# A fused attention and mixture-of-adapters kernel: moved key/value rows, moved counts, exchanged PSUM banks and a new order of the last chunks

## The chip, the cores and the metric

The kernel runs on one core of one Trainium2 chip. The metric is the time of one execution on the device in microseconds (us); the median of several runs is compared. All times inside an execution come from one profiled execution and count from the start of its span.

## The reference

Attention over spatially pooled keys and values, and then a mixture of low-rank adapters on its result. q is 4 x 12288 x 128 (batch, rows, channels) and kv is 4 x 384 x 32 x 128.

```
kv_pool = kv.reshape(B, H//4, 4, W//4, 4, C).mean(axis=(2, 4))   # 768 rows per batch
k = v   = kv_pool.reshape(B, 768, C) @ w_sr
x       = softmax(q @ k.T / sqrt(C)) @ v
logits  = x @ w_gate                        # 8 experts
w       = softmax over the two largest logits
out     = x + sum over these two e of  w[e] * (x @ A[e]) @ B[e]   # A[e] 128x16, B[e] 16x128
```

x has 4 x 12288 = 49152 rows; all inputs and the output are fp32.

## The kernel before

**The chunks.** The rows of q are handled in 96 chunks of 512 rows, 24 to a batch. The source numbers batches from 0; the words "batches 3 and 4" mean those with the numbers 2 and 3, the last two. One pass of the main loop (line 686, `for c in range(2, NCH - 1)`) does one stage for each of several chunks, so that each engine always has work: scores of a chunk ahead, weighing of chunk c-1, the turn of x of chunk c-2, and the adapters of a chunk some 6 to 9 back. The order of instructions on each engine is the order in which the source issues them (the scheduler is manual), and an instruction waits in its engine's queue until its operands and its buffer are ready; everything behind it on this engine waits too.

**One chunk, in order.** SyncE (SP) issues the loads of q and their transposes. TensorE (PE) does three times two score matmuls (`next_scores`, line 628; matmuls L329), each pair into one of two "sg" buffers of two PSUM banks, and ScalarE makes exp of them (L330). PE weighs values with these exponentials (`weigh`, L341, 24 matmuls in two halves) into the pair of banks "x". The values carry eight columns more: seven hold the gate logits relative to the eighth, and a column of ones gives the softmax's sum. VectorE (DVE) normalises x of the chunk (reciprocal L348, multiplication into `xn_all` L352) and takes the largest logits (MAX8, L359). GpSimd (POOL) makes the argument of the gate from them (L368 to L372) and casts q (L108). PE turns the upper halves of x into bf16 columns (`turned`, L408) in the bank "tp", and VectorE copies them out (`evacuate`, L419).

**The adapters.** ScalarE makes tanh of the gate's argument, VectorE transposes it (`send_gates`, L428), SP stores it to a buffer `g_h` in DRAM (L429), and `load_gates` (L436) loads it back, repeated over the adapters' 16 rows, as `ge`. `gated_hidden` multiplies x with A (L443, one matmul into the bank "hd" or one that is given) and VectorE multiplies with the gates, into `ht` (L446). `up` multiplies `ht` with B (L489, four matmuls, `d_ps`, into "hd" or a bank that is given); `give` adds x on VectorE (L503) and SP stores a pair of chunks (L522). In a usual chunk PE's order is: scores, first half of the weighing, scores, `up` of an old chunk into "hd", second half of the weighing, a step of key/value preparation if one is due, the turn of x into "tp", scores, `gated_hidden` into "hd".

**The lag.** `LAGS` (line 675) says how many chunks later the hidden layer of a chunk runs: 9 at first, then 8 from chunk 57, 7 from chunk 67, 6 from chunk 81. Where the lag falls, a pass has two hidden layers (65, 74 and 87) or two up-projections (69, 78 and 91). The loop issues the additional one in the place of the up-projection (lines 704 to 707), and one of the two takes the bank "tp":

```
for x in made.get(c, ())[:-1]:
    gated_hidden(x, t_bank())
for x in ups.get(c, ()):
    up(x, None if x == ups[c][-1] else t_bank())
```

**PSUM.** All eight banks are taken in the loop: "tp" and "hd" one buffer of one bank each, "x" one buffer of two banks, "sg" two buffers of two banks.

**Keys and values.** `plan(b)` (line 279) writes, by hand, in which pass the twelve rows of kv of a batch are loaded by SP (`at`; `load_row`, L87, 512 KB each), summed on POOL (`sm`; L194, L198 and L199), and pooled, made values and keys on PE and ScalarE (`st`; L210, L218, L226), relative to the first pass of the batch before. `prep` (rows and sums) comes near the end of a pass, `prep_step` after the weighing. POOL's `squares` (L265, L269) and VectorE's `ranges` (L272, L273) sum the squares of values and of gate columns, for a test of their size. `count_ok` (L553, L555, L558), `values_ok` (L561 to L563) and `count_sum` (L568 to L572) count in passes 82 to 86 whether all softmax sums and values so far are in the range that the fast formulas need; `ranges` stand in passes 32, 40, 56 and 80. All of these stand ahead of the last `gated_hidden` of a pass and of VectorE's copy of x.

**The last chunks.** After the loop the source issues the rest by hand (lines 757 to 909, n = 95 is the last chunk), with other banks, and with the gates applied by token instead of by row (`gate_args`, `gate_tanh`, `gate_w`, `gated`). `x_first` puts x into the bank of an up-projection by four small matmuls with the identity (L481), in which case ScalarE only copies the sum out (`take`); without it VectorE adds x (`add_rows`, L503). The last chunk is handled in two halves: two rows of tokens by `x_first` and ScalarE, two by VectorE. `all_ok` (L580 to L584) makes the flag `bad`, which every engine reads; a slow general path under `tc.If(bad_v != 0)` isn't taken here.

## Time and profile before

| What | Value |
|---|---|
| Median of the three runs shown | 374.38 us |
| Lowest and highest of them | 373.61 and 374.59 us |
| The profiled execution's own time | 374.13 us |
| Its span (first to last instruction) | 372.2 us |
| Mean granted TensorE clock | 0.999 |
| Passes of the main loop | 93 (chunks 2 to 94) |

The profile gives for each engine the busy share of the span, the chain of work that ended last, and groups of instructions by source line. In a row of the timeline, the first number is the start in microseconds from the start of the span, the second the busy time, then come engine, source line, operation, output<-inputs, shape and count, and in brackets how long the engine stood idle before it and what released it. "SPq" is SyncE issuing a transfer, "DMA" the transfer itself. Rows that count (x12) hold that many instructions in one.

### The profile page before, as it was taken

The numbers are of one execution on the slowest core, as the hardware profiler recorded it, in microseconds if no ns is written. First come the engines' busy times: TensorE is split into PE (matmuls) and PEld (weight loads), VectorE is DVE, ScalarE is ACT, GpSimd is POOL, SyncE is SP. The second block draws the span as 40 slices with busy tenths as digits, with TensorE's granted clock in tenths as the row PEclk, the third lists the DMA queues.
The fourth block names the chain that finished last, engine by engine and source line by source line (L and its number), as shares of the span: only waits on it lengthen the run. The fifth ranks groups of instructions, "written<-read, shape, count | busy, mean of one in ns | idle before, by whom it ended". The sixth has DMA issues, their size and how long they took to land.

```text
span 372.2 us, 10593 instructions
## 1 busy us (share of the span) xinstructions
PE 357.0 (96%) x3945; PEld 263.1 (71%) x3945; DVE 300.3 (81%) x953; ACT 308.8 (83%) x390; POOL 223.5 (60%) x374
## 2 busy tenths in 40 slices
PE   3889999999999899999999999999999999999985
PEld 1556777777777677777777777777777777677773
DVE  3785558888888788888888888888888889988994
ACT  1679998989889798988988988988888888879844
POOL 1022799988799787755679787755534324323243
PEclk9999999999999999999999999999999999999999
DMA  7999999999999999999999999998778799745324
GB/s 275 421 342 228 308 302 308 304 319 298 293 349 319 278 303 335 230 326 309 306 302 375 273 333 283 258 308 236 242 210 269 225 229 238 223 119 142 146 114 173
DMA packets 83818, 101.01 MB, mean 271 GB/s; under 512 B 58804, under 2 KB 59060, under 8 KB 83764
## 3 DMA queue, kind: packets, MB, share of 16 engines
q1 hardware_dynamic: 83332, 99.98, 94.3%
q8 instruction: 31, 0.51, 0.6%
q10 hardware_dynamic: 432, 0.33, 0.3%
q14 instruction: 23, 0.19, 0.2%
HBM read 62.33 MB, written 25.90 MB: 237 GB/s over the span
## 4 chain that ended last, share of the span: by engine, by line
PE 87%; DVE 5%; DMA 3%; ACT 3%; issue 1%; POOL 1%; SPq 0%; ACTq 0%; DVEq 0%
PE xps L341 34%; PE sg L329 31%; PE t_ps L408 5%; PE d_ps L489 5%; PE h_ps L443 5%; PE w_ps L609 2%; DMA ge<-g_h 2%; ACT tt L330 2%; PE v_ps L218 1%; DMA w_gate_sb<-in_moe_w_gate_dram 1%; DVE xn_all L352 1%; DVE ht L446 1%; DVE osb L503 1%; PE k_ps L243 1%; ACT qT L597 0%
## 5 line engine op out<-in xcount | busy, mean ns | idle before, releaser
L330 ACT ACTIVATE tt<-sg 128x1024 f16<-128x1024 f32 x288 | 276.9, 1022 | 36.5 <-PE sg L329 35.5
L329 PE MATMUL sg<-qT,kfT 128*128 128x512 f16 x576 | 170.2, 379 | 0.5 <-ACT qT L597 0.3
L341 PEld LDWEIGHTS <-tt 128*128 128x128 f16 x2304 | 146.1, 98 | 28.4 <-DVE xn_all L352 18.1
L341 PE MATMUL xps<-vext,tt 128*128 128x136 f16 x2256 | 164.7, 223 | 0.3 <-DVE xn_all L352 0.2
L503 DVE TENSOR_TENSOR osb<-d_ps,xn_all 128x512 f32<-128x512 f32 x85 | 58.7, 691 | 28.9 <-PE d_ps L489 27.8
L368 POOL TENSOR_TENSOR arg<-xn_all,top 128x64 f32<-128x64 f32 x47 | 14.4, 306 | 100.2 <-DVE top L359 80.6
L352 DVE TENSOR_TENSOR xn_all<-xps,rinv_all 128x540 f32<-128x540 f32 x94 | 67.7, 720 | 3.3
L329 PEld LDWEIGHTS <-kfT 128*128 128x128 f16 x576 | 49.2, 98 | 24.6 <-issue 1.8
L194 POOL TENSOR_TENSOR kvt<-kvt 128x1024 f32<-128x1024 f32 x27 | 63.6, 2357 | 2.7 <-DMA q<-in_q_dram 2.6
L108 POOL CAST q<-q 128x1024 f16<-128x1024 f32 x45 | 46.8, 1040 | 23.4 <-DMA q<-in_q_dram 23.4
L446 DVE SCALAR_TENSOR_TENSOR ht<-ge,h_ps 128x512 bf16<-128x512 f16 x87 | 58.5, 673 | 1.9 <-DMA ge<-g_h 1.4
L489 PEld LDWEIGHTS <-ht 128*128 128x128 bf16 x368 | 27.0, 98 | 25.1 <-DVE ht L446 6.1
L359 DVE MAX8 top<-xn_all 128x8 f32<-128x8 f32 x376 | 35.0, 156 | 6.3
L419 DVE COPY xt<-t_ps 128x512 bf16<-128x512 bf16 x92 | 36.8, 400 | 0.0
L408 PE MATMUL t_ps<-id_bf,xn_all 128*128 128x128 bf16 x376 | 36.3, 219 | 0.0
L489 PE MATMUL d_ps<-b_bf,ht 128*128 128x128 bf16 x340 | 32.9, 219 | 1.2 <-DVE ht L446 1.2
L443 PE MATMUL h_ps<-xt,a_bf 128*128 128x512 bf16 x87 | 33.0, 379 | 0.1
L348 DVE RECIPROCAL rinv_all<-xps 128x4 f32<-128x4 f32 x94 | 17.1, 182 | 12.9 <-PE xps L341 11.5
L408 PEld LDWEIGHTS <-xn_all 128*128 128x128 bf16 x376 | 25.9, 98 | 0.3
L371 POOL TENSOR_SCALAR msk<-msk 128x64 f32<-128x64 f32 x47 | 20.1, 428 | 4.1
L372 POOL TENSOR_TENSOR arg<-arg,msk 128x64 f32<-128x64 f32 x47 | 15.0, 319 | 3.9
L370 POOL TENSOR_TENSOR arg<-arg,msk 128x64 f32<-128x64 f32 x47 | 15.0, 319 | 3.7
(152 smaller groups left out, 220.4 us busy)
## 6 DMA issues: line engine op xcount, KB each, us to landing
kvt<-in_kv_dram SPq DMA_DIRECT2D x48, 512.0 KB
q<-in_q_dram SPq DMA_DIRECT2D x46, 512.0 KB
out_dram<-osb SPq DMA_DIRECT2D x44, 512.0 KB
ge<-g_h SPq DMA_DIRECT2D x45, 256.0 KB
out_dram<-osb SPq DMA_DIRECT2D x7, 256.0 KB
q<-in_q_dram SPq DMA_DIRECT2D x1, 1024.0 KB
qT<-q SPq DMA_TRANSPOSE x46
g_h<-g_sb SPq DMA_DIRECT2D x45, 16.0 KB
```

Source lines behind the costliest of these rows:

```text
L108: nc.gpsimd.tensor_copy(q16[i], q32[i].rearrange("p k n -> p (k n)"))
L194: eng.tensor_tensor(v[:, 0], v[:, 0], v[:, d], op=ALU.add)
L329: mm(sg[:, k], kfT[b][:, j * P:(j + 1) * P], qc, start=True, stop=True)
L330: nc.scalar.activation(tt[c][:, 2 * r:2 * r + 2], sg, AF.Exp, bias=0.0, scale=scale)
L341: mm(o, tt[c][:, j, s * P:(s + 1) * P], vext[b][:, j, 0:VW], start=(j == 0 and s % 2 == 0), stop=(j == NJ - 1 and s % 2 == 1), skip_group_ ...
L352: nc.vector.tensor_tensor(xn[c][:, :, 0:C + G].rearrange("p (b s) v -> p b s v", b=2), xv[:, :, :, 0:C + G], ri.rearrange("p (b s) -> p b ...
L408: mm(columns(t_ps, c, s), src[:, s], id_bf, is_transpose=True, start=(s == 0), stop=(s == NS - 1), skip_group_check=True)
L419: nc.vector.tensor_copy(to, t_ps)
L443: mm(h_ps, a_bf, xT[c], start=True, stop=True)
L446: nc.vector.scalar_tensor_tensor(hgT[c].rearrange("p (k a) t -> p k (a t)", k=2), gE[c // 2][:, h:h + NS // 2].rearrange("p a t k -> p k ( ...
L489: mm(dps[c][:, s], columns(hgT[c], c, s), b_bf, start=(s == 0 and fresh), stop=(s == NS - 1), skip_group_check=True)
L503: nc.vector.tensor_tensor(osb[:, lo:hi], d, xn[c][:, lo:hi, 0:C], op=ALU.add)
```

## The change

There are four edits.

1. In `plan`, for the batches with the numbers 2 and 3, the rows of kv are loaded, summed and used two passes later (`sm`, `st`); the loads (`at`) lie two passes apart, but for one pair (the ninth and tenth row, in the same pass). The passes of `squares` move by two as well (`k0`).
2. `ranges`, `count_ok`, `values_ok` and `count_sum(1)` come at the end of a pass, behind the last `gated_hidden`, `send_gates` and VectorE's copy of x.
3. In a pass with two hidden layers, the first goes to "hd" and the up-projection that follows to "tp" (before: "tp" and "hd"). In a pass with two up-projections, the first goes to "hd" and the second to "tp" (before: "tp" and "hd").
4. After the loop: chunk n-2 gets its x by `x_first`, two rows of tokens early and two late, and is copied out by ScalarE; the gate of chunk n runs on VectorE (`last_args`, `gate_w`) but for its mask on POOL; one turn is split into its matmuls (`turned_in`) and its copy (`fetch`); chunk n isn't halved any more: `up(n)` goes to "tp", VectorE adds x to all of it, and one store follows on ScalarE's queue; `all_ok` comes last, in the bank "hd".

```diff
@@ -283,9 +283,9 @@
             sm = [3, 5, 6, 8, 9, 10, 12, 14, 16]
             st = [10, 14, 19]
         else:
-            at = [-11, -9, -7, -5, -5, -3, -1, 1, 1, 3, 5, 7]
-            sm = [-3, -1, 1, 3, 5, 7, 9, 11, 13]
-            st = [4, 10, 16]
+            at = [-9, -7, -5, -3, -1, 1, 3, 5, 7, 7, 9, 11]
+            sm = [-1, 1, 3, 5, 7, 9, 11, 13, 15]
+            st = [6, 12, 18]
         for i, k in enumerate(at):
             loads.setdefault(c0 + k, []).append((b, i // 4, i % 4))
         for i, k in enumerate(sm):
@@ -701,10 +701,11 @@
         next_scores()
         if c in tanhs:
             gate_tanhs(tanhs[c])
-        for x in made.get(c, ())[:-1]:
-            gated_hidden(x, t_bank())
+        two = len(made.get(c, ())) > 1
+        if two:
+            gated_hidden(made[c][0])
         for x in ups.get(c, ()):
-            up(x, None if x == ups[c][-1] else t_bank())
+            up(x, t_bank() if two or x != ups[c][0] else None)
             give(x)
         if c in fetched and lag(2 * fetched[c] + 1) <= 8:
             load_gates(fetched[c])
@@ -722,20 +723,11 @@
             _, evacuate_h = turned("h", c - 4, stile("t_ps")[:, 0])
         next_scores()
         prep(c)
-        k0 = 19 if b == 0 else 17
+        k0 = 19
         if k in (k0, k0 + 2, k0 + 4) and b + 1 < B:
             if b == 0:
                 squares(0, (k - k0) // 2)
             squares(b + 1, (k - k0) // 2)
-        if c in (32, 40, 56, 80):
-            ranges((32, 40, 56, 80).index(c))
-        a = slice(0, CUT * NS)
-        if CUT < c <= CUT + 3:
-            count_ok(a, c - CUT - 1, flags[:, 0:1])
-        elif c == CUT + 4:
-            values_ok()
-        elif c == CUT + 5:
-            count_sum(1)
         for x in made.get(c, ())[-1:]:
             gated_hidden(x)
         if c in sent:
@@ -747,6 +739,16 @@
         if c == NCH - 2:
             evacuate_h(True)
 
+        if c in (32, 40, 56, 80):
+            ranges((32, 40, 56, 80).index(c))
+        a = slice(0, CUT * NS)
+        if CUT < c <= CUT + 3:
+            count_ok(a, c - CUT - 1, flags[:, 0:1])
+        elif c == CUT + 4:
+            values_ok()
+        elif c == CUT + 5:
+            count_sum(1)
+
 
 
     score_banks.close()
@@ -767,6 +769,17 @@
         eng.tensor_tensor(a, a, m, op=ALU.add)
         eng.tensor_scalar(m, m, 0.0, None, op0=ALU.is_ge)
 
+
+    def last_args():
+        lg = xn[n][:, :, C:C + E]
+        bc = [P, NS, E]
+        t1, t2 = (top5[:, :, i].unsqueeze(2).broadcast_to(bc) for i in range(2))
+        nc.gpsimd.tensor_tensor(msk5, lg, t2, op=ALU.subtract)
+        nc.gpsimd.tensor_scalar(msk5, msk5, 0.0, None, op0=ALU.is_ge)
+        nc.vector.tensor_tensor(arg5, lg, t1, op=ALU.subtract)
+        nc.vector.tensor_tensor(tmp5, lg, t2, op=ALU.subtract)
+        nc.vector.tensor_tensor(arg5, arg5, tmp5, op=ALU.add)
+
     def gate_tanh(lo, hi, arg):
         nc.scalar.activation(arg[:, lo:hi], arg[:, lo:hi], AF.Tanh, bias=0.0, scale=0.5)
 
@@ -786,19 +799,23 @@
             hb.rearrange("p s (r e) -> p s r e", e=E),
             g[:, lo:hi].unsqueeze(2).broadcast_to([P, hi - lo, RK, E]), op=ALU.mult)
 
-    def turn(src, lo, hi, bank_, store, key, act=True):
...
+    def turned_in(src, bank_):
...
+    def fetch(t_ps, store, key, act=True):
...
+    def turn(src, bank_, store, key, act=True):
+        fetch(turned_in(src, bank_), store, key, act)
     def high(c):
         return xn[c].bitcast(U16)[:, :, 1:2 * C:2].bitcast(BF16)
@@ -816,8 +833,9 @@
     top4, top5 = top[:, 0:NS], top[:, NS:2 * NS]
     pair = xn_all[:, q_ % 5]
     xn[n - 1], xn[n] = pair[:, 0:NS], pair[:, NS:2 * NS]
-    arg4, msk4, arg5, msk5 = (
-        small.tile([P, NS, E], FP32, tag=f"r{i}", name=f"r{i}", bufs=1) for i in range(4))
+    arg4, msk4, arg5, msk5, tmp5 = (
+        small.tile([P, NS, E], FP32, tag=f"r{i}", name=f"r{i}", bufs=1) for i in range(5))
+
     def tops4(c, top, y):
         ri = rinv_all[:, c]
         xv = y[:, :, 0:2 * VW].rearrange("p b (s v) -> p b s v", v=VW)
@@ -851,6 +869,7 @@
     up(n - 6, bank(1))
     o6 = take(n - 6)
     h2 = hidden(n - 3, 0, NS, mtile([P, NTOK], name="h2"))
+    x_first(n - 2, fbank(0), 0, 2)
     up(n - 5, bank(0))
     gate_args(n - 1, 0, NS, nc.gpsimd, top4, arg4, msk4)
     y5 = ps_e.tile([P, 2, 512], FP32, tag="y5", name="y5")
@@ -859,7 +878,7 @@
     put(n - 5, add_rows(n - 5))
     add(n - 6, o6, nc.gpsimd)
     put(n - 6, o6)
-    turn(high(n - 1), 0, NS, bank(1), xT, n - 1)
+    turn(high(n - 1), bank(1), xT, n - 1)
     h3 = hidden(n - 2, 0, NS, t_bank())
     gated(n - 2, 0, NS, gw[q_ - 1][:, NS:2 * NS], h3)
     weigh(n, 1)
@@ -869,44 +888,36 @@
     gate_w(0, NS, nc.gpsimd, arg4, msk4)
     tops4(n, top5, y5)
     tail_ok()
-    turn(hg[n - 3], 0, NS, mtile([P, NTOK], name="t2"), hgT, n - 3)
+    turn(hg[n - 3], mtile([P, NTOK], name="t2"), hgT, n - 3)
     h4 = hidden(n - 1, 0, NS, bank(1))
-    turn(hg[n - 2], 0, NS, t_bank(), hgT, n - 2)
-    turn(high(n), 0, NS, bank(0), xT, n)
-    gate_args(n, 0, NS, nc.gpsimd, top5, arg5, msk5)
+    last_args()
+    t_3 = turned_in(hg[n - 2], t_bank())
+    turn(high(n), bank(0), xT, n)
+    x_first(n - 2, None, 2, 4)
+    up(n - 3, mtile([P, NTOK], name="d2"))
     gate_tanh(0, NS, arg5)
-    up(n - 3, mtile([P, NTOK], name="d2"))
-    x_first(n - 1, fbank(1), 0, 2)
+    fetch(t_3, hgT, n - 2)
     gated(n - 1, 0, NS, arg4, h4)
-    up(n - 2, fbank(0))
-    put(n - 3, add_rows(n - 3))
-    put(n - 2, add_rows(n - 2))
+    gate_w(0, NS, nc.vector, arg5, msk5)
     x3 = ps_e.tile([P, 2, 512], FP32, tag="y5", name="x3")
     h5 = hidden(n, 0, NS, x3[:, 0])
-    turn(hg[n - 1], 0, NS, bank(1), hgT, n - 1)
-    gate_w(0, NS, nc.gpsimd, arg5, msk5)
     gated(n, 0, NS, arg5, h5)
-    x_first(n - 1, fbank(1), 2, 4)
+    add(n - 4, o1, nc.gpsimd)
+    put(n - 4, o1)
+    put(n - 3, add_rows(n - 3))
+    turn(hg[n - 1], bank(1), hgT, n - 1)
+    x_first(n - 1, fbank(1), 0, 2)
+    up(n - 2)
+    o3 = take(n - 2)
+    put(n - 2, o3)
+    turn(hg[n], bank(0), hgT, n, False)
+    x_first(n - 1, None, 2, 4)
     up(n - 1)
     o4 = take(n - 1)
     put(n - 1, o4)
-    add(n - 4, o1, nc.gpsimd)
-    put(n - 4, o1)
-    d5 = as_tokens(x3[:, 1])
-    for s in range(2):
-        mm(d5[:, s], id_f32, xn[n][:, s, 0:C], start=(s == 0), stop=False, skip_group_check=True)
-    turn(hg[n], 0, 2, bank(0), hgT, n)
-    turn(hg[n], 2, 4, t_bank(), hgT, n, False)
-    all_ok(bank(1))
-    for s in range(2):
-        mm(d5[:, s], hgT[n][:, s], b_bf, start=False, stop=(s == 1), skip_group_check=True)
-    o5 = half_out()
-    nc.scalar.activation(o5[:, 0:2], d5[:, 0:2], AF.Copy)
-    d6 = as_tokens(mtile([P, NTOK], name="d6"))
-    for s in range(2, 4):
-        mm(d6[:, s - 2], hgT[n][:, s], b_bf, start=(s == 2), stop=(s == 3), skip_group_check=True)
-    nc.vector.tensor_tensor(o5[:, 2:4], d6[:, 0:2], xn[n][:, 2:4, 0:C], op=ALU.add)
-    put(n, o5, queue=nc.scalar)
+    up(n, t_bank())
+    put(n, add_rows(n), queue=nc.scalar)
+    all_ok(mtile([P, NTOK], name="cnt"))
 
     end_banks.close()
     ps_g = ctx.enter_context(tc.tile_pool(name="ps_g", bufs=1, space=bass.MemoryType.PSUM))
```

18 lines of the change are left out of this document (9 added, 9 removed).

## The prediction

> **What bounds the kernel now.** I read the page from the top, then the chain of work that ended last, then the timelines of PE, DVE and SP around the chunks that the edits touch.
>
> ```profile
> span 372.2 us, 10593 instructions
> PE 357.0 (96%) x3945; PEld 263.1 (71%) x3945; DVE 300.3 (81%) x953; ACT 308.8 (83%) x390; POOL 223.5 (60%) x374
> PEclk9999999999999999999999999999999999999999
> DMA  7999999999999999999999999998778799745324
> PE 87%; DVE 5%; DMA 3%; ACT 3%; issue 1%; POOL 1%; SPq 0%; ACTq 0%; DVEq 0%
> ```
>
> PE sets the pace: it holds 87% of the chain, and its clock is never cut. The DMA engines are nearly full until about two thirds of the span. So an edit pays only where PE waits, and such waits must be looked for one by one. A chunk in which nothing waits looks like this (I call the start of the chunk's first weighing matmul W; the next W is 281.97, quoted below):
>
> ```profile
> 278.59 0.87 PE L341 MATMUL xps<-vext,tt 128*128 128x136 f16 x12
> 279.74 0.39 PE L489 MATMUL d_ps<-b_bf,ht 128*128 128x128 bf16 x4
> 280.16 0.69 DVE L503 TENSOR_TENSOR osb<-d_ps,xn_all 128x512 f32<-128x512 f32 x1 [0.40 <-PE d_ps L489]
> 281.08 0.72 DVE L352 TENSOR_TENSOR xn_all<-xps,rinv_all 128x540 f32<-128x540 f32 x1
> ```
>
> The reader is to see: d_ps at W+1.15, VectorE's add at W+1.57 after 0.40 us of idle, xn_all done at W+3.21, the next W at W+3.38. PE is back to back, and VectorE has some tenths to spare. Every chunk that takes over 3.38 us plus its own extra matmuls has a wait in it.
>
> **The change part by part.** *1. The kv rows.* The one long PE wait of the loop:
>
> ```profile
> 120.39 6.86 DMA ge<-g_h
> ...
> 127.34 0.69 DVE L446 SCALAR_TENSOR_TENSOR ht<-ge,h_ps 128x512 bf16<-128x512 f16 x1 [1.43 <-DMA ge<-g_h]
> ...
> 126.31 0.59 PE L329 MATMUL sg<-qT,kfT 128*128 128x512 f16 x2
> 128.09 0.40 PE L489 MATMUL d_ps<-b_bf,ht 128*128 128x128 bf16 x4 [1.18 <-DVE ht L446]
> ...
> 105.17 0.57 SPq L436 DMA_DIRECT2D ge<-g_h  x1
> 111.66 0.58 SPq L436 DMA_DIRECT2D ge<-g_h  x1
> 113.44 1.45 SPq L87 DMA_DIRECT2D kvt<-in_kv_dram  x2
> 120.39 0.59 SPq L436 DMA_DIRECT2D ge<-g_h  x1
> ```
>
> d_ps should follow the start of the two sg matmuls by 0.43 us (they are 0.216 apart), so at 126.74; it came at 128.09: 1.34 us lost. It waited for ht, ht for the gates' load, and that load was issued late: SP passed from one gates load to the next in 6.5 us where one kv row lay between, and in 8.7 us where two did (113.44), while two chunks of PE take 6.8 and, with a pooling step in them, a little more. One row in two chunks keeps pace; each second row costs about 1.5 us of lead. The old plan has such pairs in chunks 13 (with the batch before), 19 and 25; the new one has none before chunk 31, so three rows fewer, some 4.5 us of queue, lie ahead of the load that was 1.4 us late. I take this wait as gone: **-1.34**. What is late next: the pair in chunk 31 and the rows in 33 and 35, where the old plan had none; they give the lead back only in part, since the total of rows issued is at no chunk above the old total. Bounds: -1.34 and 0. Each moved row, an SP issue of about 0.6 us, is put behind two more chunks' gates, q, transposes and output stores, which pass it by. Around batch 4's rows no wait for a load stands now, and they move the same way. The sums on POOL move with the pooling on PE; for the later rows the lead of a load over its sum shrinks from six chunks to four, 13.5 us, twice what the late gates load took to land (6.86). Pooling, value and key steps, and the squares on POOL, move by two chunks; their work stays the same.
>
> *2. The counts behind the copy.*
>
> ```profile
> 317.14 0.87 PE L341 MATMUL xps<-vext,tt 128*128 128x136 f16 x12
> 317.36 0.48 DVE L555 SCALAR_TENSOR_TENSOR ok<-rinv_all,ok 128x324 f32<-128x324 f32 x1
> 317.76 0.68 DVE L446 SCALAR_TENSOR_TENSOR ht<-ge,h_ps 128x512 bf16<-128x512 f16 x1
> 318.50 0.40 PE L489 MATMUL d_ps<-b_bf,ht 128*128 128x128 bf16 x4
> ...
> sum 17.72, DVE 16.50; mean DVE 3.30
> ```
>
> The count stands ahead of ht; h_ps's bank comes free only at 318.44, and d_ps starts at W+1.36 instead of W+1.15. The last row is the sum of the five chunks that hold such a wait and no other extra (three with ranges, two with counts): 17.72 - 5 x 3.38 = 0.82 us. A sixth, with the flags of the values, has the same order beside two small matmuls of its own; I count it as the mean of the five, 0.16. All of that, 0.98, of which I take **-0.95**, goes when ht and the copy come first. What covers the counts then is VectorE's idle time ahead of the add (0.40 in a chunk without a gates transpose, about 0.25 with one). The longest, 0.48 to 0.5 us, overruns it by about 0.1 to 0.2; xn_all would end at W+3.3 to 3.4, and the next weighing needs it some 0.05 before W+3.38. So up to 0.05 comes back in each chunk: bounds -0.98 and -0.65.
>
> *3. The banks at lag changes.* Six chunks have a second hidden layer (65, 74, 87) or a second up-projection (69, 78, 91).
>
> ```profile
> 281.97 0.87 PE L341 MATMUL xps<-vext,tt 128*128 128x136 f16 x12
> 282.20 0.67 DVE L446 SCALAR_TENSOR_TENSOR ht<-ge,h_ps 128x512 bf16<-128x512 f16 x1
> 282.91 0.38 DVE L419 COPY xt<-t_ps 128x512 bf16<-128x512 bf16 x1
> 283.35 0.38 PE L443 MATMUL t_ps<-xt,a_bf 128*128 128x512 bf16 x1
> 283.76 0.69 DVE L446 SCALAR_TENSOR_TENSOR ht<-ge,t_ps 128x512 bf16<-128x512 f16 x1 [0.47 <-PE t_ps L443]
> 284.37 0.68 DVE L503 TENSOR_TENSOR osb<-d_ps,xn_all 128x512 f32<-128x512 f32 x1
> 284.50 0.38 PE L408 MATMUL t_ps<-id_bf,xn_all 128*128 128x128 bf16 x4
> 285.95 0.88 PE L341 MATMUL xps<-vext,tt 128*128 128x136 f16 x12
> ...
> sum 23.21, DVE 19.69; mean DVE 3.28
> ```
>
> Today the first hidden layer waits for the copy out of the "tp" bank: 283.35 instead of 283.12, 0.23 late. With the exchange it goes to the "hd" bank, free at 282.87, and that wait is gone. But "tp" is then held by the up-projection, whose reader is the *second* VectorE operation of the stage. The turn of x (L408), next in PE's order, writes "tp" and must wait for that reader; today it waits for the first, which ends at 284.45, just in time. New times from W: hidden layer 1.15, ht at 1.15 + 0.41 = 1.56 (0.41 as from 283.35 to 283.76), add 0.61 later at 2.17, its end 2.85, turn of x at 2.90 (0.05 for the handover). PE alone would be there at 1.15 + 0.22 + 0.22 + 0.71 = 2.30. From the turn to the next W it takes 1.30 (285.95 - 284.50 less the 0.15 for which that W waited for xn_all). So the chunk takes 4.20. With two up-projections both places hold an add, and the same sum gives 4.20. The last row is the sum of the six chunks now: 23.21. Six times 4.20 is 25.20, less 0.11 for the keys' turn that now falls into chunk 69 under the wait: **+1.9**. Queued behind the turn are the scores, so ScalarE's exponentials start late too, but they have a chunk of lead. Bounds: +2.3 if each of the six loses 0.05 more at its handovers, and, if the turn did not wait at all, 6 x 3.60 - 23.21 = -1.6.
>
> *4. The last chunks.*
>
> ```profile
> 358.97 0.72 DVE L825 TENSOR_TENSOR xn_all<-y,rinv_all 128x540 f32<-128x540 f32 x1
> 360.11 0.38 PE L489 MATMUL e<-b_bf,ht 128*128 128x128 bf16 x4 [0.46 <-ACT ht L417]
> 363.37 0.37 DVE L830 MAX8 top<-xn_all 128x8 f32<-128x8 f32 x4
> 363.99 0.66 PE L481 MATMUL f<-xn_all,id_f 128*128 128x128 f32 x4
> 365.32 0.25 POOL L779 TENSOR_TENSOR r<-r,r 128x32 f32<-128x32 f32 x1
> 365.61 0.69 DVE L784 TENSOR_TENSOR hgs<-x,r 128x512 bf16<-128x512 f32 x1
> 367.87 0.20 DVE L584 TENSOR_SCALAR bad<-last,tot 1x1 int32<-1x1 f32 x1
> 368.65 0.36 ACTq L508 DMA_DIRECT2D out_dram<-osb  x1
> ```
>
> The new half of x_first(n-2) can start only when xn_all is done (359.69) and takes 0.5 us (four matmuls at 363.99; the next group follows 0.5 later), so it ends near 360.22 where 360.11 was due: +0.11 for all behind it. The last chunk's gates now run on VectorE: three operations of 32 elements behind MAX8, for which VectorE shows no row; MAX8's four take 0.37 in all and POOL's operation of this size 0.25 each, so between 0.3 and 0.75; I take 0.5 with handovers. Their gated hidden layer of chunk n-1 follows near 364.30, the weight at 364.9, and the last gating runs 365.12 to 365.80, where it now runs 365.61 to 366.30. Then the add of n-3 to 366.40, the copy of the last turn 366.38 to 366.78 (0.4 as other copies), four up matmuls to 367.27, the full add of 0.69 to 367.98, the store at 368.03: 0.62 earlier than 368.65. Against that, the flag "bad" now comes after the add, at about 368.44, where it was ready at 368.07, and every engine reads it before the program ends. From the last store to the end of the span go 372.2 - 368.65 = 3.55 us, from the flag at most 372.2 - 368.07 = 4.13. If the store decides: -0.62; if the flag does: up to +0.37. Between them I take **-0.3**.
>
> *Sum:* -1.34 - 0.95 + 1.9 - 0.3 = -0.7. The profiled execution took 374.13; 373.4 after it. It lies 0.25 under the median of the runs shown, 374.38, so **373.6**, 0.2% faster; about 0.3% (1.1 us) is what a measurement of this kernel can tell from no change.
>
> **The rivals.** *The exchange does what its two moves look like:* the turn finds its bank free. For it: the wait at 283.35 is real. Against: one "tp" bank, and VectorE's order, in which the second reader comes second. Then part 3 gives -1.6 and the time is 374.38 - 4.2 = 370.2.
>
> *The gates' load stays late:* the queue is as full at the new places, part 1 gives 0: 374.9. Against: the row totals.
>
> *It ends slower:* the rows in chunks 31, 31, 33 and 35 follow each other without the free pairs that the old plan had there. If the queue comes to chunk 31 as full as it now comes to 25, loads for chunks 34, 36 and 38 are late by about 1.4, 1.0 and 1.0: 373.6 + 3.4 = 377.0. It decides from the point where a gates load takes over 7 us to land. Against: three rows fewer by then.
>
> *The clock:* new waits of 0.6 us inside six chunks could cost TensorE its clock.
>
> ```profile
> 126.00:129.00 3.00, 1.82 (x27) 1.33 (x24) 1.50 (x3) 2.24 (x4) 2.58 (x2) 1.00 1.02 359
> ```
>
> The row says that PE stood idle for 1.2 us of these 3 and kept a granted clock of 1.00. One chunk at half the clock would take 3.4 more: 377.0. The Trainium skill, TensorE: Matmul & The Clock Gate, section "A second HAM failure mode: psum-queue depth-cycling", tells of a kernel in which short idles between groups of matmuls, as it cycled through PSUM banks, made the clock fall and rise again. By that rule the exchange, which adds just such idles, would be paid by the clock as well; this trace's longest idle of the loop speaks against it.
>
> **How the numbers follow.** Forecast 0.66, its own range 372.9 to 374.4; exchange free 0.10; load still late 0.15; slower by the queue 0.07; clock 0.02. The range leaves out the free exchange and the two slow cases (0.19); below the forecast it takes in part 4 at its best (-0.3) and a third of the way to part 3's lower bound (-1.2), above it the late load (374.9) and 0.3 for the upper ends of parts 2 and 4: 372.0 to 375.2 with the rounding. Faster by over 0.3% (under 373.26): 0.10 and some 0.20 of the forecast's lower end, 0.30. Slower (over 375.5): 0.09. Within: 0.61.
>
> **What would show it.** Chunk 30 at 3.9 us instead of 5.24, no DMA releaser before ht (part 1); chunks behind ranges and counts at 3.38 to 3.45 (part 2); six chunks at about 4.2, with PE's t_ps at L408 released by osb (part 3); the last store 0.5 to 0.6 earlier, the span by less (part 4). Wrong if the six stay at 3.6, or if VectorE waits for ge after chunk 33.

## The result and the profile after

The changed kernel takes 375.26 us in the median of 18 runs (374.62 to 375.87), the kernel before 374.23 us in 18 runs beside it: a ratio of 1.0029 (95% interval 1.0021 to 1.0038), 0.8 to 1.4 us slower. The prediction was 373.6 with a range of 372.0 to 375.2. The profiled execution took 374.93 us, its span is 373.0 against 372.2.

The page of the changed kernel: span, busy times, and the shares of the chain that ended last (here and below, a fence holds chosen rows of its view).

```profile
span 373.0 us, 10606 instructions
PE 356.2 (95%) x3949; PEld 264.9 (71%) x3949; DVE 301.0 (81%) x956; ACT 308.3 (83%) x389; POOL 222.9 (60%) x370
...
PE 88%; DVE 5%; ACT 2%; issue 1%; DMA 1%; POOL 1%; ACTq 0%; DVEq 0%
```

DMA's share of the chain fell from 3% to 1%: the wait of part 1 is gone. PE did 0.8 us less, and yet the span grew. To see where, I cut the span at two points that both kernels have: the first weighing of chunk 1 (30.19 before, 30.48 after; the part ahead of it isn't touched by the change) and that of the last chunk, by its rows of the timeline, first of the kernel before:

```profile
360.33 0.87 PE L341 MATMUL y<-vext,tt 128*128 128x136 f16 x12
```

and of the changed one:

```profile
360.26 0.87 PE L341 MATMUL y<-vext,tt 128*128 128x136 f16 x12
```

| Stretch | before | after | difference |
|---|---|---|---|
| start to chunk 1 | 30.19 | 30.48 | +0.29 |
| chunk 1 to the last chunk | 330.14 | 329.78 | -0.36 |
| last chunk to the end of the span | 11.87 | 12.74 | +0.87 |

The middle stretch also holds 0.25 us that edit 4 adds ahead of the last weighing (part 4 below). So edits 1 to 3 took about 0.6 from the loop, where 0.4 was forecast, and edit 4 lost more than they won.

**Part 1 in the timeline of the changed kernel** (chunk 30, and SP's loads of gates for it and the next; as in the prediction, a chunk of the loop is named by its pass):

```profile
125.67 0.87 PE L341 MATMUL xps<-vext,tt 128*128 128x136 f16 x12
125.90 0.67 DVE L446 SCALAR_TENSOR_TENSOR ht<-ge,h_ps 128x512 bf16<-128x512 f16 x1
126.81 0.39 PE L489 MATMUL d_ps<-b_bf,ht 128*128 128x128 bf16 x4
129.27 0.87 PE L341 MATMUL xps<-vext,tt 128*128 128x136 f16 x12
...
117.19 0.57 SPq L436 DMA_DIRECT2D ge<-g_h  x1
123.94 0.56 SPq L436 DMA_DIRECT2D ge<-g_h  x1
```

`ht` names no releaser, d_ps stands at W+1.14, and SP needs 6.75 us from one gates load to the next. The chunk takes 3.60, which is 3.38 and a pooling step; before, with a values step in it, it took 5.24, which is 1.35 over another chunk with such a step (3.89).

**Part 2** (chunk 84, where `count_ok` cost 0.23 before):

```profile
316.66 0.87 PE L341 MATMUL xps<-vext,tt 128*128 128x136 f16 x12
316.88 0.67 DVE L446 SCALAR_TENSOR_TENSOR ht<-ge,h_ps 128x512 bf16<-128x512 f16 x1
317.60 0.38 DVE L419 COPY xt<-t_ps 128x512 bf16<-128x512 bf16 x1
317.80 0.39 PE L489 MATMUL d_ps<-b_bf,ht 128*128 128x128 bf16 x4
317.90 0.49 DVE L555 SCALAR_TENSOR_TENSOR ok<-rinv_all,ok 128x324 f32<-128x324 f32 x1
320.03 0.87 PE L341 MATMUL xps<-vext,tt 128*128 128x136 f16 x12
```

The count now lies between the copy and the add, and the chunk takes 3.37. All five chunks are free of extra time, the sixth fell from 3.78 to 3.61. No kernel below undoes edit 2 alone: its size is read from these chunks.

**Part 3** (chunk 74):

```profile
281.23 0.87 PE L341 MATMUL xps<-vext,tt 128*128 128x136 f16 x12
282.37 0.38 PE L443 MATMUL h_ps<-xt,a_bf 128*128 128x512 bf16 x1
283.39 0.68 DVE L503 TENSOR_TENSOR osb<-t_ps,xn_all 128x512 f32<-128x512 f32 x1
284.13 0.38 PE L408 MATMUL t_ps<-id_bf,xn_all 128*128 128x128 bf16 x4 [0.43 <-DVE osb L503]
285.43 0.34 PE L341 MATMUL xps<-vext,tt 128*128 128x136 f16 x3
```

The six chunks in the view by windows, the row of chunk 74 and the sum:

```profile
281.23:285.43 4.20, 3.77 (x41) 2.68 (x40) 3.90 (x16) 2.87 (x4) 0.00 (x0) 1.00 0.67 184
...
sum 25.22, PE 22.68 PEld 16.60 DVE 22.24 ACT 18.43 POOL 11.01; mean PE 3.78 PEld 2.77 DVE 3.71 ACT 3.07 POOL 1.84
```

The hidden layer starts at W+1.14, the add ends at W+2.84, and the turn of x, released by that add, starts at W+2.90, as worked out. The chunk takes 4.20, the six 25.22 instead of 23.21. In the row by window the granted clock (the number before the DMA share) is 1.00.

**Part 4.** The view of the chain lists its longest steps. The last of them in the changed kernel is one that the kernel before doesn't have:

```profile
358.65 0.73 DVE xn_all L843
362.55 0.73 DVE xn_all L843
364.80 0.93 DVE r L789
```

(The chain itself goes on to the flag, L584. It is followed back from the last busy instruction of an engine, and the landing of a store is none; so whether flag or store sets the end is read from SP's waits below.) L789 is the gate weight of the last chunk on VectorE, 32 elements wide. In the timeline:

```profile
359.52 0.68 PE L481 MATMUL f<-xn_all,id_f 128*128 128x128 f32 x4 [0.19 <-DVE xn_all L843]
360.04 0.39 PE L489 MATMUL e<-b_bf,ht 128*128 128x128 bf16 x4
364.09 0.19 DVE L781 TENSOR_TENSOR r<-r,r 128x32 f32<-128x32 f32 x1
364.40 1.27 POOL L498 TENSOR_TENSOR osb<-osb,xn_all 128x512 f32<-128x512 f32 x1
364.80 0.92 DVE L789 SCALAR_TENSOR_TENSOR r<-r,r 128x32 f32<-128x32 f32 x1
365.82 0.69 DVE L797 TENSOR_TENSOR hgs<-x,r 128x512 bf16<-128x512 f32 x1
368.68 0.36 ACTq L508 DMA_DIRECT2D out_dram<-osb  x1
368.79 0.20 DVE L584 TENSOR_SCALAR bad<-last,tot 1x1 int32<-1x1 f32 x1
```

The first row is the new half of `x_first`, ahead of the last weighing: it starts 0.14 behind the end of `xn_all` (358.65 and 0.73), where the prediction left 0.03, and the last chunk's first weighing comes 4.55 us behind that of the chunk before it, where it was 4.30.

An operation of the size of L789 took 0.19 just before it (L781). L789 took 0.92 and ended at 365.72, with POOL's addition for chunk n-4 (364.40 to 365.67). The change had put that addition ahead of the last gating; in the kernel before POOL made the gate weight itself and came to the addition only behind it. So the last gating started at 365.82, and nothing of the forecast's 0.6 us was left.

The last store was issued at 368.68, 8.42 us behind the last chunk's first weighing where it was 8.32. But from there to the end of the span go 4.32 us, not 3.55. SP's waits at the end, before:

```profile
SPq L1032 <- DMA out_dram<-osb: 0.8, 2, 0.6
```

and after:

```profile
SPq L1043 <- DMA out_dram<-osb: 1.0, 1, 1.0
```

In both kernels SP still waits for a store when it has long read the flag: the store decides the end. Why it lands later is in the row of the DMA engines, forty slices of 0.125 us from 367 to 372, before:

```profile
DMA  9601010008999999999889998970030000000000
```

and after:

```profile
DMA  8810000289898589999999999999997402000000
```

In the kernel before three stores were issued in the last 1.5 us of issuing (367.17, 367.76, 368.65), now four are (367.14, 367.93, 368.40, 368.68). Each is 256 KB, 0.69 us of all sixteen DMA engines by the times of its packets, and they are busy to 370.9 instead of 370.4.

### The profile page after: what moved, and what is told of

The parts are those of the page before. It is cut to its first block, busy times and chain, and to the rows that moved or that the text cites. A ratio compares the mean times of both kernels' runs of the same rounds, so it can differ in the third digit from the quotient of the medians.

```text
span 373.0 us, 10606 instructions
## 1 busy us (share of the span) xinstructions
PE 356.2 (95%) x3949; PEld 264.9 (71%) x3949; DVE 301.0 (81%) x956; ACT 308.3 (83%) x389; POOL 222.9 (60%) x370
## 4 chain that ended last, share of the span: by engine, by line
PE 88%; DVE 5%; ACT 2%; issue 1%; DMA 1%; POOL 1%; ACTq 0%; DVEq 0%
PE xps L341 34%; PE sg L329 32%; PE t_ps L408 6%; PE h_ps L443 5%; PE d_ps L489 5%; PE w_ps L609 2%; DVE osb L503 2%; ACT tt L330 2%; PE v_ps L218 1%; DMA w_gate_sb<-in_moe_w_gate_dram 1%; DVE ht L446 1%; PE k_ps L243 1%; DVE hgs L797 0%; PE kp_ps L210 0%; ACT qT L597 0%
## 5 line engine op out<-in xcount | busy, mean ns | idle before, releaser
L503 DVE TENSOR_TENSOR osb<-d_ps,xn_all 128x512 f32<-128x512 f32 x82 | 56.7, 692 | 32.1 <-PE d_ps L489 32.1
L446 DVE SCALAR_TENSOR_TENSOR ht<-ge,h_ps 128x512 bf16<-128x512 f16 x90 | 60.5, 672 | 1.3 <-PE h_ps L443 0.9
L443 PE MATMUL h_ps<-xt,a_bf 128*128 128x512 bf16 x90 | 34.1, 379 | 0.1
L489 PE MATMUL d_ps<-b_bf,ht 128*128 128x128 bf16 x328 | 31.7, 219 | 0.0
```

Source lines behind the costliest of these rows:

```text
L443: mm(h_ps, a_bf, xT[c], start=True, stop=True)
L446: nc.vector.scalar_tensor_tensor(hgT[c].rearrange("p (k a) t -> p k (a t)", k=2), gE[c // 2][:, h:h + NS // 2].rearrange("p a t k -> p k ( ...
L489: mm(dps[c][:, s], columns(hgT[c], c, s), b_bf, start=(s == 0 and fresh), stop=(s == NS - 1), skip_group_check=True)
L503: nc.vector.tensor_tensor(osb[:, lo:hi], d, xn[c][:, lo:hi, 0:C], op=ALU.add)
```

## The experiments

Each kernel was compared with the kernel before on the same chip; "W" of the last chunk is its first weighing matmul.

| Kernel | median us | before | 95% interval of the ratio |
|---|---|---|---|
| e1_loop_only | 373.95 | 374.26 | 0.9976 to 1.0002 |
| e2_tail_only | 374.86 | 374.26 | 0.9993 to 1.0031 |
| e4_add_late | 375.02 | 374.26 | 1.0012 to 1.0036 |
| e5_store_early | 374.89 | 374.26 | 1.0004 to 1.0031 |
| e6_no_store | 374.25 | 374.31 | 0.9982 to 1.0008 |
| e7_banks_old | 373.36 | 374.31 | 0.9960 to 0.9983 |
| e8_pe_adds | 374.95 | 374.31 | 1.0005 to 1.0030 |
| e9_swap | 372.63 | 374.31 | 0.9929 to 0.9968 |
| e10_swap_old_tail | 371.70 | 374.18 | 0.9899 to 0.9954 |
| e11_swap_new_tail | 372.37 | 374.18 | 0.9925 to 0.9967 |
| e12_plan_old | 375.1 (one run) | 374.18 | - |
| e13_swap_plan_old | 372.90 | 373.87 | 0.9958 to 0.9983 |

**Is it the loop or the last chunks?** Two kernels split the change: edits 1 to 3 alone, and edit 4 alone (everything behind the loop). They have no lines of their own, only the hunks of the change.

> Edits 1 to 3 with the last chunks as before. Theory (the loop did what was forecast, the loss is in the last chunks): chunk 30 -1.35, counts -1.00, six exchanged chunks +1.84, so 0.5 us under the kernel before, and the stretch from the last chunk's weighing to the end 11.9 us as before. Rival 1 (the last chunks only show a lateness that the loop or the start makes): as the changed kernel, 1.0 us over the kernel before. Rival 2 (the exchange costs less than its periods show): 2 us under.

> Edit 4 alone, with the main loop as before. Theory: +0.25 for the half of x_first ahead of the last weighing and +0.87 behind it, so 1.1 us over the kernel before; the gate weight on VectorE takes 0.9 us and ends with POOL's addition, as in the changed kernel. Rival 1 (the loss is not in the last chunks): within 0.3 of the kernel before. The prediction's own sum for this edit was -0.3.

The loop edits alone: 0.31 under the kernel before (interval 0.9 under to 0.1 over), 0.43 less in the profile between chunk 1 and the end. That is the theory's 0.5; rival 1 is out. Behind the last weighing it takes 12.1 us, where 11.9 was expected. Edit 4 alone: 0.6 over, with an interval from 0.3 under to 1.2 over, so the median by itself doesn't decide. Its profile has the same 0.92 us in the gate weight and the same 0.25 ahead of the last weighing, but the end came 12.14 us behind the last chunk's first weighing, not 12.74. Here the store of n-2 was issued 0.4 earlier (7.29 us behind W instead of 7.67), the last store landed sooner, and SP shows no wait for it at the end any more. The flag, at 8.52 us behind W (8.53 in the changed kernel), was followed by the end 3.6 later; that end lies 0.27 above the 11.87 of the kernel before. That is not a floor: in the changed kernel SP came to its wait for the store early enough that without this wait of 1.0 us the end would lie at 11.7, under those 11.87. Why SP needed longer from the flag on in this run no run shows.

**Why 0.92 us for the gate weight?** One small POOL operation on the mask holds POOL's addition back until VectorE has read the mask:

```diff
     gated(n, 0, NS, arg5, h5)
+    nc.gpsimd.tensor_scalar(msk5, msk5, 0.0, None, op0=ALU.is_ge)
     add(n - 4, o1, nc.gpsimd)
-    put(n - 4, o1)
     put(n - 3, add_rows(n - 3))
...
     put(n - 2, o3)
+    put(n - 4, o1)
```

> The changed kernel, but POOL's addition for chunk n-4 is held back until VectorE has made the gate weight of chunk n (a small POOL operation that rewrites the mask stands ahead of it), and that chunk's store goes behind the one of n-2. Theory (the two engines can't both read SBUF, the later one waits): the gate weight takes 0.2 us instead of 0.92, the last gating starts at about 4.9 us after the last chunk's first weighing instead of 5.56, the last store is issued 0.6 earlier; the end comes 0.3 to 0.6 earlier, since five stores now stand close together. Rival (an operation of this form takes 0.9 us by itself): 0.92 again, and no change of the time.

```profile
365.39 0.18 DVE L789 SCALAR_TENSOR_TENSOR r<-r,r 128x32 f32<-128x32 f32 x1
365.68 0.69 DVE L797 TENSOR_TENSOR hgs<-x,r 128x512 bf16<-128x512 f32 x1
365.90 1.28 POOL L498 TENSOR_TENSOR osb<-osb,xn_all 128x512 f32<-128x512 f32 x1
368.58 0.39 ACTq L508 DMA_DIRECT2D out_dram<-osb  x1
```

The same operation takes 0.18 without POOL's addition beside it; the last gating stands at 4.82 us behind W (360.86) instead of 5.56, the store of the last chunk at 7.72 instead of 8.42. The rival, a slow operation, is out. The end came only 0.2 earlier. Now the store of n-4 stands among the last five, and that of the last chunk landed 3.5 us behind its issue: the time was won on the engines and lost in the DMA engines. The Trainium skill, SBUF — State Buffer, section "Who interferes with whom", has the rule: a VectorE instruction with two inputs in SBUF (where all tiles lie that aren't in PSUM) and a GpSimd instruction that reads SBUF don't run together, the later one waits until the first is done; a VectorE instruction with at most one input in SBUF isn't concerned, outside the modes in which VectorE uses both of its ports. Both halves are seen here: L789 with two SBUF inputs, 0.92 against 0.18, and the gating L797, one of whose inputs is in PSUM, beside POOL's addition in this run: 0.69 and 1.28 us, neither longer than in the changed kernel by more than 0.01. The rule spoke against moving POOL's addition to this place, and the prediction didn't draw on it.

**Does the backlog of stores decide the end?** Two tries, one with the stores reordered, one with a store left out.

```diff
-    put(n - 3, add_rows(n - 3))
+    o2 = add_rows(n - 3)
...
     put(n - 2, o3)
-    turn(hg[n], bank(0), hgT, n, False)
+    put(n - 3, o2)
     x_first(n - 1, None, 2, 4)
     up(n - 1)
     o4 = take(n - 1)
     put(n - 1, o4)
+    turn(hg[n], bank(0), hgT, n, False)
```

> The changed kernel, with the stores of the last chunks earlier: n-2 ahead of n-3, and the up-projection, copy and store of n-1 ahead of the turn of the last hidden layer. The gate weight stays as it is. Theory (the last store lands late because the stores ahead of it fill the DMA engines): the last store is issued at the same point, lands 0.6 to 0.7 earlier, and the time falls by as much, to 0.4 over the kernel before. Rival (the flag, which is ready 0.3 us behind the last store's issue, decides the end): no change, 1.0 over the kernel before.

```diff
     o4 = take(n - 1)
-    put(n - 1, o4)
```

> The changed kernel without the store of chunk n-1, whose rows stay unwritten (256 KB less to write, nothing else changed). Theory (the last store lands late because the stores issued just ahead of it, 0.69 us of all DMA engines each, are still under way): the last store lands 2.6 to 2.7 us behind its issue, as in the kernel before, instead of 3.3, and the end is then set by the flag, 3.6 behind it: 0.6 us less than the changed kernel, 0.4 over the kernel before. Rival (the landing of this store varies by itself): 3.3 again, no change.

The first is inconclusive: SP took 0.90 us to issue the store of n-2 (0.33 is usual), and so the store of n-1 left at 8.25 us behind W, no earlier than in the changed kernel (8.14). The median is 0.4 under that of the changed kernel; in the profile, taken in the slowest of its twelve runs, the end is not earlier. The second leaves the rows of n-1 in the output unwritten, and is clear. The DMA row from 367 to 372, with the last store issued at 368.82:

```profile
DMA  9982000008999964999994899992000120000000
```

The engines are done at about 370.4, 1.6 us behind the issue, against 1.7 in the kernel before (368.65 to 370.4) and 2.2 in the changed one. SP's wait for the store at the end fell to half:

```profile
SPq L1042 <- DMA out_dram<-osb: 0.5, 1, 0.5
```

By the semaphore updates in the traces the last store landed 2.61 us behind its issue, against 3.34 in the changed kernel and 2.63 in the kernel before. The end came 12.1 us behind W instead of 12.7, and the median is 1.0 us under that of the changed kernel, level with the kernel before. (That the flag would then set the end didn't come true: SP still waits for the store.) The last chunks' loss in the profile, 0.87, is by this the backlog (0.7) and the later issue (0.1).

But how many stores stand close together isn't all of it. In `e2_tail_only` and `e12_plan_old` the same four stores are issued in the last 1.5 us, with that of n-2 at 7.29 us behind W, and the last one landed after 2.63 and 2.54 us. In the changed kernel, `e7_banks_old` and `e9_swap` that store left at 7.65 to 7.67, and the last one landed after 3.34 to 3.36. The first two are the kernels with the old rows; why SP issues this store sooner in them no run shows.

**What does the exchange of banks cost?** Edit 3 undone,

```diff
-        two = len(made.get(c, ())) > 1
-        if two:
-            gated_hidden(made[c][0])
+        for x in made.get(c, ())[:-1]:
+            gated_hidden(x, t_bank())
         for x in ups.get(c, ()):
-            up(x, t_bank() if two or x != ups[c][0] else None)
+            up(x, None if x == ups[c][-1] else t_bank())
```

> The changed kernel without edit 3: banks at the lag changes as before. Theory: the six chunks at 3.75 to 3.98 again instead of 4.20, 1.84 us less than the changed kernel, 0.8 under the kernel before. Rival (the time lost in these chunks is made up behind them, by the exponentials that wait there or in the last chunks): less than 0.6 of it comes back.

and edit 3 carried to its end:

```diff
...
+    swapped = [False]
+    def hidden_bank():
+        return t_bank() if swapped[0] else mtile([P, NTOK], name="h_ps")
+    def turn_bank():
+        return mtile([P, NTOK], name="t_ps") if swapped[0] else t_bank()
...
-        two = len(made.get(c, ())) > 1
-        if two:
-            gated_hidden(made[c][0])
+        if len(made.get(c, ())) > 1:
+            gated_hidden(made[c][0], hidden_bank())
         for x in ups.get(c, ()):
-            up(x, t_bank() if two or x != ups[c][0] else None)
+            two = len(made.get(c, ())) > 1 or x != ups[c][0]
+            up(x, turn_bank() if two else hidden_bank())
             give(x)
+        if len(made.get(c, ())) > 1 or len(ups.get(c, ())) > 1:
+            swapped[0] = not swapped[0]
...
-        _, evacuate = turned("x", c - 2)
+        _, evacuate = turned("x", c - 2, turn_bank())
...
-            gated_hidden(x)
+            gated_hidden(x, hidden_bank())
```

> The changed kernel, but at each lag change the two banks change places for good: the turn of x and all later turns take the bank whose reader comes first, the last hidden layer and all later ones the other; after six changes the places are the old ones again. Theory (the turn waits for the second VectorE reader of its bank): the turn of the six chunks starts at 2.3 us instead of 2.9, and the chunks take 3.7 to 3.9, since VectorE then has about 3.6 us of work in them; 1.8 to 2.4 less than the changed kernel, about 1 under the kernel before. Rival (it waits for something else): 4.20 again. Rival 2 (nothing is left to wait for): 3.60.

Undone, the time falls by 1.9 (375.26 to 373.36), what the six chunks cost in the profile. With the places changed for good (chunk 74 of that kernel):

```profile
280.80 0.87 PE L341 MATMUL xps<-vext,tt 128*128 128x136 f16 x12
283.11 0.39 PE L409 MATMUL t_ps<-id_bf,xn_all 128*128 128x128 bf16 x4
283.77 0.72 DVE L352 TENSOR_TENSOR xn_all<-xps,rinv_all 128x540 f32<-128x540 f32 x1
284.55 0.53 PEld L341 LDWEIGHTS <-tt 128*128 128x128 f16 x9 [0.47 <-DVE xn_all L352]
284.55 0.47 PE L341 MATMUL xps<-vext,tt 128*128 128x136 f16 x5
```

and by windows:

```profile
sum 22.51, PE 22.51 PEld 15.94 DVE 19.70 ACT 19.20 POOL 10.58; mean PE 3.75 PEld 2.66 DVE 3.28 ACT 3.20 POOL 1.76
```

The turn starts at W+2.31 without a wait, and all six chunks take 3.75: 2.7 us less than in the changed kernel, a little more than the 1.8 to 2.4 expected, and 0.7 less than before. The chunk shown doesn't take 3.60, since VectorE has two more operations to do and is done with `xn_all` only at 284.49, and the weight load of the next weighing waits for it (the row with 0.47 us of idle). The prediction's rival "exchange free", 6 x 3.60, counted PE alone: this kernel, where the turn doesn't wait, comes to 22.51, not 21.6.

**Can the last chunks be mended?** First with x of chunk n-4 added by TensorE, so that POOL reads nothing beside L789:

```diff
-    up(n - 4, bank(0))
     gate_tanh(0, NS, arg4)
-    o1 = take(n - 4)
...
     last_args()
-    t_3 = turned_in(hg[n - 2], t_bank())
+    x_first(n - 4, fbank(1), 0, 4)
+    up(n - 4)
     turn(high(n), bank(0), xT, n)
+    t_3 = turned_in(hg[n - 2], t_bank())
...
     fetch(t_3, hgT, n - 2)
+    o1 = take(n - 4)
...
-    add(n - 4, o1, nc.gpsimd)
...
+    up(n - 2)
     x_first(n - 1, fbank(1), 0, 2)
-    up(n - 2)
```

> The changed kernel, but x is added to chunk n-4 by four matmuls of TensorE instead of by POOL, so that POOL reads nothing while VectorE makes the gate weight; the turn of hidden layer n-2 goes behind that of x of the last chunk to make room, the copy out of n-4 behind it on ScalarE. Theory: gate weight 0.2 us, last gating at about 4.9 us behind the last chunk's first weighing instead of 5.56, the last store issued at 7.8 instead of 8.4, and as no store is pushed back, the end 0.6 to 0.8 earlier: 0.3 over the kernel before. Rival (only the stores decide): as with the addition held back, 0.2 earlier.

L789 took 0.19, and the last gating stands at 5.08 us behind W (360.59), near the 4.9 expected. But the last store was issued at 8.29, not at 7.8:

```profile
365.32 0.19 DVE L789 SCALAR_TENSOR_TENSOR r<-r,r 128x32 f32<-128x32 f32 x1
366.24 0.71 PE L481 MATMUL f<-xn_all,id_f 128*128 128x128 f32 x4
366.79 0.39 PE L805 MATMUL e<-id_bf,hgs 128*128 128x128 bf16 x4
368.88 0.36 ACTq L508 DMA_DIRECT2D out_dram<-osb  x1
```

The matmuls that put x of n-1 into their bank (366.24) had to wait until ScalarE had copied n-4 out of the same bank, and the turn of the last hidden layer (366.79) stood behind them on PE. So 0.3 us were won, not 0.6 to 0.8. Then with that turn ahead, and the flag early (on top of the kernel with the changed places):

```diff
     h5 = hidden(n, 0, NS, x3[:, 0])
+    count_tail(x3[:, 1])
...
-    x_first(n - 1, fbank(1), 0, 2)
...
     turn(hg[n], bank(0), hgT, n, False)
-    x_first(n - 1, None, 2, 4)
+    all_ok(x3[:, 1])
+    x_first(n - 1, fbank(1), 0, 4)
...
-    all_ok(mtile([P, NTOK], name="cnt"))
```

> As the kernel with the banks that change places for good (edit 4 in), but with the last chunks mended by what the runs showed: x of chunk n-4 added by TensorE, so that POOL reads nothing beside the gate weight; the turn of the last hidden layer ahead of the matmuls that put x of n-1 into their bank; the counts' matmuls in an idle moment of TensorE and the flag ahead of the last addition. Theory: last gating at 5.1 us behind the last chunk's first weighing, last store issued at 7.8 instead of 8.4, flag at 7.4 instead of 8.5, end at 11.4 to 12.0 instead of 12.75: 2.5 to 3.0 us under the kernel before. Rival (the stores' backlog alone decides, however early they are issued): 12.5, 1.9 under.

```profile
363.33 0.69 DVE L811 TENSOR_TENSOR hgs<-x,r 128x512 bf16<-128x512 f32 x1 [0.46 <-PE x L582]
366.63 0.36 ACTq L509 DMA_DIRECT2D out_dram<-osb  x1
```

This expectation failed: the counts' matmuls stand in the same PSUM tile as the last hidden layer, and the gating now waits for them (0.46 us); the last store left at 8.68 us behind W. The end lies 12.5 us behind W and the time 1.8 under the kernel before, the numbers of the rival; but the rival speaks of stores that leave earlier, and these left later, so it wasn't put to the test. 372.37 is 0.3 under `e9_swap` as the two stand, 0.1 when each is taken against the kernel before beside it, and still slower than with the old last chunks (the same loop, without edit 4's hunks):

> Edits 1 and 2, the banks that change places for good, and the last chunks as before (no edit 4). Theory (the loss behind the loop is edit 4's own): from the last chunk's first weighing to the end 11.9 us instead of 12.75, and 0.25 less ahead of it, so about 1.0 less than with edit 4: 2.6 us under the kernel before. Rival (a faster loop makes the old last chunks late as well): as with edit 4, 1.7 under.

371.70 us, 2.5 under the kernel before (ratio 0.9926, interval 0.9899 to 0.9954): edits 1 and 2, the banks changed for good, no edit 4. It is the fastest kernel of this study. Beside e9_swap it gives the price of edit 4 again: 0.9 us, or 0.8 when each is taken against the kernel before beside it.

**Edit 1** was undone in two kernels, the changed one and e10_swap_old_tail:

```diff
-            at = [-9, -7, -5, -3, -1, 1, 3, 5, 7, 7, 9, 11]
-            sm = [-1, 1, 3, 5, 7, 9, 11, 13, 15]
-            st = [6, 12, 18]
+            at = [-11, -9, -7, -5, -5, -3, -1, 1, 1, 3, 5, 7]
+            sm = [-3, -1, 1, 3, 5, 7, 9, 11, 13]
+            st = [4, 10, 16]
...
-        k0 = 19
+        k0 = 19 if b == 0 else 17
```

> The changed kernel without edit 1 (rows, sums and steps of the last two batches as before), one look. Theory (each second row in two chunks costs SP about 1.5 us, and three such pairs make the load of gates for chunk 30 late): this load takes over 6 us to land again and chunk 30 has 1.2 to 1.4 us of wait in it, that is 5.1 to 5.3 us; nothing else of the loop changes. Rival (the counts or the start set the lateness, not the rows): chunk 30 at 3.9.

```profile
125.83 0.87 PE L341 MATMUL xps<-vext,tt 128*128 128x136 f16 x12
126.89 0.69 DVE L446 SCALAR_TENSOR_TENSOR ht<-ge,h_ps 128x512 bf16<-128x512 f16 x1 [0.74 <-DMA ge<-g_h]
130.39 0.81 PE L341 MATMUL xps<-vext,tt 128*128 128x136 f16 x11
```

The wait is back at the same place, but the chunk takes 4.56, 0.67 over 3.89, not the 5.1 to 5.3 expected; and chunk 36, which had no such wait before, takes 3.99, 0.10 over. What the old rows cost thus changes from one execution to the next, and I asked the median:

> Edit 2, the banks that change places for good and the last chunks as before, without edit 1: what edit 1 is worth in the median, beside the kernel that has it too (371.7). The wait in chunk 30 was 1.35, 1.25 and 0.67 us in three profiles with the old rows. Theory (the load of gates is late by an amount that changes from execution to execution, 1.1 on average): 1.1 over the kernel with edit 1, 1.4 under the kernel before, and a wider spread of the runs. Rival 1 (1.34 each time, as forecast): 1.2 under. Rival 2 (the wait is made up later or is a feature of few executions): less than 0.5 over the kernel with edit 1, 2.0 or more under.

Against 371.70 with the new rows, 372.90 without: 1.2 us, or 1.5 when each is taken against the kernel before beside it. That is well over rival 2's half microsecond. It doesn't tell the theory's 1.1 from the forecast's 1.34: the time is 1.0 under the kernel before (0.6 to 1.6), where the one said 1.4 and the other 1.2; the runs spread over 1.8 us, those with the new rows over 1.4. This kernel's own profile, its fastest run, has a wait of 0.03 only. The four profiles with the old rows and a chunk 30 to compare have 1.35 (the kernel before), 1.25 (e2), 0.67 and 0.03; of those with the new rows none has any.

## Why the prediction was wrong

- **Part 1, right.** Forecast -1.34; -1.35 in the two profiles, 1.2 to 1.5 in the medians. It is a wait whose size varies (0.03 to 1.35 in four profiles); that a forecast from one profile, which had it at its longest, comes this close is in part luck. No load came late behind chunk 30, so the rival of the queue fell, and that of a load that stays late too.
- **Part 2, right.** Forecast -0.95; -1.00 (0.82 in five chunks, 0.17 in the sixth). The cover, VectorE's idle time ahead of the add, held. Its size stands on the chunks of the profile alone.
- **Part 3, right, mechanism and size.** Forecast +1.9; +2.01 in the six chunks, less 0.17 for the keys' turn (0.11 in the forecast): +1.84. The kernel without it is 1.9 faster, and the kernel in which the turn takes the bank with the first reader has no wait there.
- **The clock, right that it stays.** The six new idles (0.33 to 0.45 us each by the view by windows) left the granted clock at 1.00 in each of the six windows; the rule of the Trainium skill, TensorE: Matmul & The Clock Gate, section "A second HAM failure mode: psum-queue depth-cycling", which the prediction weighed, isn't borne out by idles of this length.
- **Part 4, wrong, and with it the sign.** Forecast -0.3; in the profile +0.25 ahead of the last weighing and +0.87 behind it, between 0.6 and 1.3 us in the medians (e2 beside the kernel before 0.6, e9 beside e10 0.9, the changed kernel beside e1 1.3). Three steps failed. First, the gate weight: "so between 0.3 and 0.75; I take 0.5 with handovers" and "the weight at 364.9" took its price from rows of its size, some 0.2 us, and didn't ask what POOL does at that time. The change also moves POOL's addition there, and the weight waited for its end: 0.92 against 0.18. That cost 0.74, all of the gain of 0.6. Second, "From the last store to the end of the span go 372.2 - 368.65 = 3.55 us" was taken as a constant. It is the time that the store needs behind those ahead of it, and here it grew by 0.7; without the store of n-1 that 0.7 was gone, and it was absent as well in the two kernels whose store of n-2 left 0.4 earlier. Third, the half of `x_first` ahead of the last weighing cost 0.25, not 0.11.
- **The flag.** The prediction's case "if the flag does: up to +0.37" came near only in e2, where the store lands early: +0.27. In the changed kernel SP ends with a wait for the store, and its way from the flag alone would have added nothing.

The sum by measured terms is -1.2 - 1.0 + 1.84 + 0.9, that is +0.5, with the 1.12 of the profile for edit 4 instead of the 0.9 it is +0.8; the medians differ by 1.03 (0.8 to 1.4). What is left stays open: the price of edit 4 is known to a few tenths only, and it seems to hang on the rows (0.6 beside the old ones, 0.8 to 1.3 beside the new ones), which the landing of the last store would explain but no run isolates.

## What to carry to other kernels

Before an operation is moved to VectorE, or a GpSimd operation to another place, write down what the other of the two reads at that time: here, with two SBUF inputs on VectorE, the price was the rest of GpSimd's operation (0.92 us), not that of the own one (0.18). At the end of a kernel, look at what is still under way ahead of the last store: issued nearly as early as before, it landed 3.3 us behind its issue instead of 2.6, and the kernels that differ in this differ by 0.4 us in the issue of an earlier store. Where a bank is exchanged to take away a wait, look for the next writer of the bank that was taken instead, and for the order of its readers; giving the roles away for good, and not for one pass, removed the wait on both sides.

## What was not expected

- The first weighing of chunk 1 lay between 30.15 and 31.26 us in the profiles of these kernels, though none changes what stands ahead of it. Single spans that differ by less than 1 us say nothing until they are cut at a common point.
- SP's issue of a 256 KB store took 0.33 us mostly, but 0.75 in e10 and 0.90 in e5; two stores that were ready left 0.4 to 0.8 us apart. How early a store is written in the program is not how early it starts.
